# Three feed-forward tiles of the first 320 rows moved into the attention stage of a fused attention, Fourier-MLP and gated-MLP kernel

## The chip, the cores and the metric

The kernel runs on one core of one Trainium2 chip. The metric is the device time of one execution in microseconds (us); lower is better. Before the change the median of three runs is 816.88 us (815.56 to 817.01).

## What is computed

Three blocks follow each other, all in float32 on 4 sequences of 576 rows and 512 features.

```python
# 1. attention, 8 heads of 64, causal, window of 64 keys
scores = q @ k.T / 8, masked to 0 <= row - col < 64
x = softmax(scores) @ v                      # heads side by side: (4, 576, 512)
# 2. Fourier mixing and an MLP
u  = x + real(fft(fft(x, axis=1), axis=2))
un = (u - mean(u)) / sqrt(var(u) + 1e-6)
x  = u + maximum(un @ w_ch1, 0) @ w_ch2      # 512 -> 2048 -> 512
# 3. gated MLP with spatial mixing
h = gelu(x @ w_in); u, v = split(h)
v = w_sg @ layernorm(v) * g + b              # over the 576 rows of a sequence
out = x + (u * v) @ w_out
```

## The kernel before, in words

**Precision.** Wide products are made of three float32r matmuls: each operand is split into a high and a low part, and `mm3` (lines 113 to 120) issues high-high, high-low and low-high. Weights arrive from memory as 8-byte words and are turned into such pairs by `decode` (lines 142 to 161): a DMA into `dec_s`, then work on ScalarE (L154, L159), VectorE (L155 to L157) and GpSimd (L160). One tile `f` of the 16 feed-forward tiles is one `set`, decoded in four pieces. `set0` to `set2` are decoded beside the attention, the others later.

**Attention** (`attention`, lines 249 to 351) goes over 36 blocks of 64 queries, `n` = 9 per sequence. A block has scores (L260, into PSUM tile `sc`), a masked maximum on VectorE (L264), exponentials on ScalarE (L268), transposes (L275, into `pt`) and their copy (L277). Every two blocks there are the products with v (L288, into `pv`), the normalization on VectorE (L303 to L307), and a transpose back (L317, into `xt`) with a copy into `uT` (L319). The stages of several blocks overlap; `LAG` says by how many steps. PSUM has eight banks. In this stage two belong to tag `g` (Fourier transform and layernorm), two to `sc`, one to `pt`, one to `xt` and two to `pv`. The keys come in tiles of three blocks (`load_k`, three buffers), the values in tiles of two blocks (`load_v`, `VB` = 3 buffers). All these loads are issued by SyncE (SP), in one fixed order with the weight loads, so a load that waits for its buffer holds up the ones behind it.

**Beside the attention** run two lanes: the decoding of tiles 0 to 2, and per sequence `dft` (lines 380 to 461) and, for the row chunks 0 and 1, `ln` (lines 487 to 521). The 2304 rows are cut into eight chunks, `n` = 0 to 7, of 320 and 256 rows in turn. `ln` leaves a chunk's normalized rows transposed in `xh` and `xl` (L519, L520). Chunk 0 is the head of sequence 0, and is ready long before the attention ends; chunk 1 is the rest of sequence 0; chunk 2 needs the transform of sequence 1.

**The MLP** (`mlp`, lines 529 to 577) begins when the attention has released its memory. `PHASES` (lines 28 and 29) lists which feed-forward tiles are made for which chunks: for each pair, 12 matmuls make `h` from `xh`, `xl` and the first weight (L564), ScalarE and VectorE turn it into `rh`, `rl` (L568, L569), and 12 matmuls add into `acc` (L544). After the last tile of a phase VectorE adds `acc` to `uT` (L549, four instructions). Lane `rest` (lines 817 to 832) runs beside it: decoding of tile 3, layernorm of chunks 2 and 3, the transforms of sequences 2 and 3, layernorm of chunks 4 to 7. Then comes the gated MLP, which the change does not touch.

**What sets the order.** The Python generators are interleaved by `drive` (lines 728 to 743) by their estimated costs. The compiler layer then schedules all instructions per engine with its own model of their times, so the order on an engine differs from the order of the source. On the chip every engine executes its list strictly in that order.

## Time and profile before

| | us |
|---|---|
| median of three runs | 816.88 |
| the profiled execution: own time | 811.93 |
| the profiled execution: span, first to last instruction | 810.2 |
| attention, until the first matmul of the MLP | 147.9 |
| TensorE busy | 777.8 (96%) |
| VectorE busy | 478.2 (59%) |
| ScalarE busy | 290.9 (36%) |
| GpSimd busy | 163.5 (20%) |

The span is what the profile's views divide up; the profiled execution's own time is 1.7 us longer. PE is TensorE's matmul row, PEld its weight loads, which overlap the matmuls, DVE is VectorE, ACT ScalarE, POOL GpSimd, SP SyncE. A matmul's end is modelled in the profile, and matmuls overlap, so a PE that reads as busy all the time can still be less than full. An "idle before" in brackets is the time in which the engine waited just before an instruction, with the instruction that ended the wait.

### The profile page before, as it was taken

The page shows a single profiled execution, that of the slowest core. Times are in us where ns is not written, and L with a number is a line of the kernel's source. Part 1 is how long each engine was busy: PE and PEld are TensorE (multiplying, and loading weights), DVE is VectorE, ACT ScalarE, POOL GpSimd, SP SyncE. Part 2 cuts the span into 40 slices and gives each one's busy share as a digit, 9 for nine tenths or more (in the row PEclk, how much of TensorE's full clock was granted, in tenths as well). Part 3 has the DMA queues.
Part 4 walks back from the last instruction along what each step waited for, and adds up shares of the span by engine and source line. Part 5 has one row for each costly group of instructions (what it writes and reads, how often), then busy time and mean ns, then how long its engine had stood idle before and what let it go on. Part 6 is the DMA issues. An engine that isn't in the chain of part 4 may idle for free.

```text
span 810.2 us, 15611 instructions
## 1 busy us (share of the span) xinstructions
PE 777.8 (96%) x6084; PEld 748.4 (92%) x6084; DVE 478.2 (59%) x1390; ACT 290.9 (36%) x710; POOL 163.5 (20%) x202
## 2 busy tenths in 40 slices
PE   5979798899999999999999999999999999999998
PEld 5779597899998999999999999999999998989898
DVE  2688978996488557963226933643240258565653
ACT  3777776442233234431113411333242243131310
POOL 1143513442031013410002300232260021010100
PEclk8999999999999999999999999999999999999999
DMA  9997631121012003420002400132140020303032
GB/s 208 295 323 224 177 97 38 61 97 53 2 40 66 1 1 105 129 82 1 1 2 69 136 6 1 34 118 85 40 134 12 0 60 1 117 1 118 1 117 93
DMA packets 59321, 63.70 MB, mean 79 GB/s; under 512 B 22384, under 2 KB 42736, under 8 KB 59248
## 3 DMA queue, kind: packets, MB, share of 16 engines
q1 hardware_dynamic: 58672, 59.75, 24.9%
q0 software_dynamic: 576, 2.97, 1.2%
q8 instruction: 48, 0.79, 0.4%
q14 instruction: 25, 0.20, 0.1%
HBM read 53.25 MB, written 9.44 MB: 77 GB/s over the span
## 4 chain that ended last, share of the span: by engine, by line
PE 74%; DVE 14%; DMA 6%; ACT 2%; issue 2%; SPq 1%; POOL 1%; DVEq 0%; ACTq 0%
PE acc L118 7%; PE acc L119 7%; PE acc L120 7%; PE h L119 6%; PE h L120 6%; PE h L118 6%; PE c L119 6%; PE c L118 6%; PE c L120 6%; PE g L118 3%; PE g L119 3%; PE g L120 3%; DMA dec_s<-in_w 2%; PE sc L260 2%; DMA dec_s<-in_wo 2%
## 5 line engine op out<-in xcount | busy, mean ns | idle before, releaser
L118 PE MATMUL acc<-rh,set 128*128 128x256 f32 (+1 forms) x512 | 151.6, 296 | 2.2 <-DVE uT L549 2.1
L118 PE MATMUL h<-xh,set 128*128 128x256 f32 (+1 forms) x512 | 151.2, 296 | 0.8 <-DVE rl L569 0.8
L119 PE MATMUL acc<-rl,set 128*128 128x256 f32 (+1 forms) x512 | 151.3, 296 | 0.0
L120 PE MATMUL acc<-rh,set 128*128 128x256 f32 (+1 forms) x512 | 151.1, 295 | 0.0
L119 PE MATMUL h<-xl,set 128*128 128x256 f32 (+1 forms) x512 | 151.0, 295 | 0.0
L120 PE MATMUL h<-xh,set 128*128 128x256 f32 (+1 forms) x512 | 150.9, 295 | 0.0
L569 DVE SCALAR_TENSOR_TENSOR rl<-h,rh 128x320 fp32r<-128x320 f32 (+1 forms) x128 | 58.1, 454 | 118.1 <-ACT rh L568 117.6
L160 POOL TENSOR_TENSOR set<-dec_w,set 128x256 fp32r<-128x256 f32 x88 | 71.9, 823 | 253.7 <-ACT set L159 250.4
L568 ACT ACTIVATE rh<-h 128x320 fp32r<-128x320 f32 (+1 forms) x128 | 51.7, 404 | 161.2 <-PE h L120 121.3
L118 PEld LDWEIGHTS acc<-rh,set 128*128 128x128 f32 x512 | 96.4, 188 | 3.6 <-issue 1.3
L118 PEld LDWEIGHTS h<-xh,set 128*128 128x128 f32 x512 | 96.3, 188 | 1.7 <-DVE rl L569 1.3
L120 PEld LDWEIGHTS acc<-rh,set 128*128 128x128 f32 x512 | 96.5, 188 | 0.1
L119 PEld LDWEIGHTS h<-xl,set 128*128 128x128 f32 x512 | 96.4, 188 | 0.1
L120 PEld LDWEIGHTS h<-xh,set 128*128 128x128 f32 x512 | 96.4, 188 | 0.0
L119 PEld LDWEIGHTS acc<-rl,set 128*128 128x128 f32 x512 | 96.4, 188 | 0.0
L549 DVE TENSOR_TENSOR uT<-acc,uT 128x320 f32<-128x320 f32 (+1 forms) x160 | 62.0, 448 | 15.2 <-PE acc L120 15.2
L154 ACT ACTIVATE dec_g<-dec_s 128x256 f32<-128x256 f32 x88 | 38.4, 438 | 78.6 <-DVE dec_w L156 37.0
L268 ACT ACTIVATE s<-s,mx 128x128 f32<-128x128 f32 x144 | 46.9, 393 | 26.4 <-DVE mx L264 26.3
L482 POOL TENSOR_TENSOR rq<-rq,mhalf 128x1 f32<-128x1 f32 (+2 forms) x26 | 17.4, 669 | 189.9 <-DVE rq L481 186.8
L155 DVE TENSOR_SCALAR dec_w<-dec_s 128x256 int32<-128x256 int32 x88 | 34.8, 398 | 35.3 <-POOL set L160 23.1
L120 PE MATMUL c<-xh,set 128*128 128x256 f32 (+1 forms) x188 | 55.4, 294 | 0.0
L118 PE MATMUL c<-xh,set 128*128 128x256 f32 (+1 forms) x188 | 55.3, 294 | 0.0
(190 smaller groups left out, 1611.9 us busy)
## 6 DMA issues: line engine op xcount, KB each, us to landing
dec_s<-in_w SPq DMA_DIRECT2D x64, 256.0 KB, 2.8
v<-in_v SPq DMA_DIRECT2D x16, 520.0 KB, 6.0
k<-in_k SPq DMA_DIRECT2D x11, 512.0 KB, 6.5
dec_s<-in_wi SPq DMA_DIRECT2D x16, 256.0 KB, 2.8
q<-in_q SPq DMA_DIRECT2D x30, 128.0 KB, 5.4
x<-uT SPq DMA_DIRECT2D x4, 640.0 KB, 3.9
out<-uT SPq DMA_DIRECT2D x4, 640.0 KB, 3.9
dec_s<-in_wo SPq DMA_DIRECT2D x8, 256.0 KB, 2.5
```

The costliest lines, as they stand in the source:

```text
L118: mm(out, lhsT=lh, rhs=rh, start=first and i == 0, stop=False)
L119: mm(out, lhsT=lh, rhs=rl, start=False, stop=False)
L120: mm(out, lhsT=ll, rhs=rh, start=False, stop=last and i == n - 1)
L154: nc.scalar.activation(out=g, in_=s[:, :, 1].bitcast(F32), func=AF.Copy, scale=2.0 ** -112)
L155: nc.vector.tensor_scalar(out=w, in0=s[:, :, 0], scalar1=29, scalar2=None, op0=ALU.logical_shift_right)
L160: (eng or nc.gpsimd).tensor_tensor(out=lo[:, o:o + 256], in0=f, in1=hi[:, o:o + 256], op=ALU.subtract)
L260: nc.tensor.matmul(sc[:, hp], lhsT=q[:, hp].rearrange("p a b -> p (a b)"), rhs=k[:, hp, o:o + 128], start=True, stop=True)
L268: nc.scalar.activation(out=s[:, hp], in_=s[:, hp], func=AF.Exp, bias=mx[:, hp:hp + 1], scale=-1.0)
L482: self.nc.gpsimd.tensor_tensor(out=y, in0=v, in1=self.mhalf[:m, 0:n], op=ALU.pow)
L549: V.tensor_tensor(out=x, in0=acc[:, c, 0:size], in1=x, op=ALU.add)
L568: A.activation(out=rh, in_=o, func=AF.Relu)
L569: V.scalar_tensor_tensor(out=rl, in0=o, scalar=0.0, in1=rh, op0=ALU.max, op1=ALU.subtract)
```

## The change

Tiles 0 to 2 of chunk 0 leave the MLP. A new generator `early` makes them beside the attention once the layernorm of chunk 0 and the decoding of tiles 0 to 2 have been issued: for each tile 12 matmuls into a PSUM tile `e`, then the ScalarE and VectorE step into `erh`, `erl`; then for each of the four feature groups 9 matmuls into `e` and one VectorE addition to `uT`. `e` has one bank. That bank comes from the rings of the attention: `sc`, `pt` and `xt` now share one ring `ab` of three banks, where they had four. `erh` and `erl` take new memory (three buffers each), and the keys and values have two buffers each in place of three; `VL` = 3 issues a load of v one step later. In `PHASES`, chunks 1 to 3 now come first with tiles 0 to 3, then chunk 0 with tiles 3 to 5, then chunks 1 to 3 with tiles 4 and 5.

```diff
--- before.py
+++ after.py
@@ -25,17 +25,19 @@
 NCH = len(CHUNKS)
 P0 = 4
 HEAD, TAIL = range(NCH // 2), range(NCH // 2, NCH)
-PHASES = [(range(P0), HEAD), (range(P0, 6), HEAD), (range(P0), TAIL), (range(P0, 6), TAIL),
+E0 = range(3)
+PHASES = [(range(P0), HEAD[1:]), (range(3, 6), HEAD[:1]), (range(P0, 6), HEAD[1:]), (range(P0), TAIL), (range(P0, 6), TAIL),
           (range(6, 10), range(NCH)), (range(10, 13), range(NCH)), (range(13, 16), range(NCH))]
 URGENT = 5000
 SOON = 6000
 RATE = 1.0
 NV = 0
-VL = 2
-LAG, XPT = (1, 2, 3), 0
+VL = 3
+LAG = 1, 2, 3
 PACE = 1.0
+EC = 5
 FP = ()
-UB, SB, QB, VB = 3, 3, 3, 3
+UB, SB, QB, VB = 3, 3, 3, 2
 WARM, W0, W1 = 16, 9000, 2500
 TAB_AT = (2, 4, 7, 9)
 DSP, D45 = 2000, 3000
@@ -202,7 +204,7 @@
         self.kt, self.vt = {}, {}
 
     def load_k(self, b, g):
-        t = self.ap_.tile([128, 4, 256], F32, tag="k", bufs=3, name="k")
+        t = self.ap_.tile([128, 4, 256], F32, tag="k", bufs=2, name="k")
         o = 192 * g
         for c in (slice(0, 128), slice(128, 256)) if b == g == 0 else (slice(0, 256),):
             self.nc.sync.dma_start(t[:, :, c], self.aps["k"][b, :, :, o + c.start:o + c.stop])
@@ -254,7 +256,7 @@
         def scores(n):
             b, j = divmod(n, NB)
             q, k = self.qt.pop((b, j)), self.kt[b, j // 3]
-            sc = ps.tile([128, 4, 128], F32, tag="sc", bufs=2, name="sc")
+            sc = ps.tile([128, 4, 128], F32, tag="ab", bufs=3, name="sc")
             for hp in range(4):
                 o = 64 * (j % 3)
                 nc.tensor.matmul(sc[:, hp], lhsT=q[:, hp].rearrange("p a b -> p (a b)"), rhs=k[:, hp, o:o + 128], start=True, stop=True)
@@ -270,7 +272,7 @@
 
         def transposes(n):
             pr = st.pop(n)
-            pt = ps.tile([128, 4, 128], F32, tag="pt", bufs=1 + XPT, name="pt")
+            pt = ps.tile([128, 4, 128], F32, tag="ab", bufs=3, name="pt")
             for hp in range(4):
                 nc.tensor.transpose(pt[:, hp], pr[:, hp], self.ident)
             pts = p.tile([128, 4, 128], F32, tag="pts", bufs=3, name="pts")
@@ -312,7 +314,7 @@
             b, j = divmod(n, NB)
             m, x = 64 if j == NB - 1 else 128, st.pop(("x", n))
             i = j // 2
-            t = ps.tile([128, 4, 128], F32, tag="pt", bufs=2, name="xt") if XPT else ps.tile([128, 4, 128], F32, tag="xt", name="xt")
+            t = ps.tile([128, 4, 128], F32, tag="ab", bufs=3, name="xt")
             for c in range(4):
                 nc.tensor.transpose(t[:, c, 0:m], x[:m, 128 * c:128 * c + 128], self.ident[:m, :m])
             t0 = S * b + 128 * i
@@ -526,6 +528,30 @@
         self.bps, es = self.pool("mlp_ps", side="right", space=PSUM)
         self.mlp_es.enter_context(es)
 
+    def early(self, n, fs):
+
+        nc, p, ps = self.nc, self.ap_, self.aps_
+        start, size = CHUNKS[n]
+        xh, xl = self.xh[n], self.xl[n]
+        hid = {}
+        for f in fs:
+            t = self.sets[f % 8]
+            o = ps.tile([128, 512], F32, tag="e", name="e")[:, 0:size]
+            self.mm3(o, [(t[:, 0, 128 * k:128 * k + 128], t[:, 1, 128 * k:128 * k + 128], xh[:, k], xl[:, k]) for k in range(4)])
+            rh = p.tile([128, CA], F32R, tag="erh", bufs=len(fs), name="erh")[:, 0:size]
+            rl = p.tile([128, CA], F32R, tag="erl", bufs=len(fs), name="erl")[:, 0:size]
+            nc.scalar.activation(out=rh, in_=o, func=AF.Relu)
+            nc.vector.scalar_tensor_tensor(out=rl, in0=o, scalar=0.0, in1=rh, op0=ALU.max, op1=ALU.subtract)
+            hid[f] = rh, rl
+            yield EC * size
+        for c in range(4):
+            s = slice(128 * c, 128 * c + 128)
+            o = ps.tile([128, 512], F32, tag="e", name="e")[:, 0:size]
+            self.mm3(o, [(self.sets[f % 8][:, 2, s], self.sets[f % 8][:, 3, s], *hid[f]) for f in fs])
+            x = self.uT[:, c, start:start + size]
+            nc.vector.tensor_tensor(out=x, in0=o, in1=x, op=ALU.add)
+            yield EC * size
+
     def mlp(self, before):
         nc = self.nc
         V, A = nc.vector, nc.scalar
@@ -764,19 +790,26 @@
             for w in gen:
                 yield w * PACE
 
+        have = set()
+
         def work():
             for b in range(2):
                 yield from when(scaled(k.dft(b)), lambda: k.xdone >= b)
                 yield from scaled(k.ln(b))
+                have.add(b)
 
         def weights():
             yield W0
             for f in range(3):
                 yield from spaced(k.decode_f(f), W1)
+            have.add("w")
+
+        def early():
+            yield from when(k.early(0, E0), lambda: have >= {0, "w"})
 
         k.open_x(0, k.lp)
         k.open_x(1, k.lp)
-        fill = [[weights()], [work()]]
+        fill = [[weights()], [work()], [early()]]
         drive(k.attention(), *fill)
         for f in sum(fill, []):
             for _ in f:
@@ -854,14 +887,14 @@
                 next(rest_)
             if n == PHASES[g][1][0]:
                 drain(lanes[1])
-                if g == 3:
+                if g == 4:
                     lanes[1].append(decodes((8, 9), 2000))
-                elif g == 4:
+                elif g == 5:
                     drain(lanes[0])
                     lanes[1].append(decodes(range(10, 13), 7000))
-                elif g == 5:
+                elif g == 6:
                     lanes[1].append(decodes(range(13, 16), 5000))
-                elif g == 6:
+                elif g == 7:
                     lanes[1].append(w_in())
 
         drive(k.mlp(before), *lanes)
```

Three places show how the order moves. A line of the changed kernel has a number two higher than the same line before in these rows (its L120 is the L118 of before).

**TensorE in the attention stage, at the second transform.** `g` is the transform, `e` the early tiles, the rest attention. Before:

```order
L120 MATMUL g<-tab,ol 128x256
L260 MATMUL sc<-k,q_97 128x128 x4
L317 MATMUL xt<-ident,x 128x64 x2
L288 MATMUL pv<-v,pts 64x65
L317 MATMUL xt<-ident,x 128x64 x2
L275 MATMUL pt<-ident,s 128x128 x4
L288 MATMUL pv<-v,pts 64x65 x15
L118 MATMUL g<-tab,oh 33x256
```

After the change, where the scores of the same part of the stage are done:

```order
L277 MATMUL pt<-ident,s 128x128 x4
L290 MATMUL pv<-v,pts 64x65 x7
L120 MATMUL e<-erh,set_69 128x320
L121 MATMUL e<-erl,set_69 128x320
L122 MATMUL e<-erh,set_69 128x320
L120 MATMUL e<-erh,set_70 128x320
L121 MATMUL e<-erl,set_70 128x320
L122 MATMUL e<-erh,set_70 128x320
L120 MATMUL e<-erh,set_71 128x320
L121 MATMUL e<-erl,set_71 128x320
L122 MATMUL e<-erh,set_71 128x320
L290 MATMUL pv<-v,pts 64x65 x9
```

The nine matmuls of one `e` group stand in the middle of a `pv` run; nothing was there before.

**TensorE where chunk 2 begins.** `h` on `xh2` is the first product of chunk 2; `g` from `u` is the last transpose of its layernorm, `acc` the MLP's sum for chunk 1. Before, the transpose is followed by chunk 1:

```order
L119 MATMUL h_2701<-xl1_113,set3_2143 128x256
L120 MATMUL h_2701<-xh1_112,set3_2143 128x256
L517 MATMUL g_2514<-ident_58,u_2385 128x64 x4
L118 MATMUL h_2701<-xh1_112,set3_2143 128x256
L119 MATMUL h_2701<-xl1_113,set3_2143 128x256
L118 MATMUL g_2521<-tab_81,oh_2310 33x256
L119 MATMUL g_2521<-tab_81,oh_2310 33x256
```

After the change the same transpose is followed at once by chunk 2:

```order
L122 MATMUL g_2583<-tab_81,ol_2406 128x256
L120 MATMUL g_2583<-tab_81,oh_2405 128x256
L121 MATMUL g_2583<-tab_81,oh_2405 128x256
L122 MATMUL g_2583<-tab_81,ol_2406 128x256
L519 MATMUL g_2592<-ident_58,u_2480 128x64 x4
L120 MATMUL h_2619<-xh2_2234,set0_69 128x320
L120 MATMUL h_2698<-xh2_2234,set1_70 128x320
L120 MATMUL g_2599<-tab_81,oh_2405 33x256
```

Before, 37 other instructions stand between that transpose and the first product of chunk 2; now none do.

**SyncE's loads near the start.** Names are those of the tiles; `dec_s` is the first weight load. Before:

```order
L233 DMA v_141<-in_v 128x2x520
L208 DMA k_143<-in_k 128x4x256
L216 DMA q2_97<-in_q 64x8x64 x2
L233 DMA v_162<-in_v 128x2x520
L216 DMA q0_95<-in_q 64x8x64 x2
L208 DMA k_204<-in_k 128x4x256
L233 DMA v_206<-in_v 128x2x520
L216 DMA q1_96<-in_q 64x4x64 x2
L208 DMA k_311<-in_k 128x4x256
L151 DMA dec_s_313<-in_w1 128x512
```

After the change:

```order
L210 DMA k_141<-in_k 128x4x256
L235 DMA v_143<-in_v 128x2x520
L218 DMA q2_97<-in_q 64x8x64 x2
L235 DMA v_177<-in_v 128x2x520
L218 DMA q0_95<-in_q 64x8x64 x2
L210 DMA k_204<-in_k 128x4x256
L218 DMA q1_96<-in_q 64x4x64 x2
L153 DMA dec_s_313<-in_w1 128x512
L153 DMA dec_s_369<-in_w1 128x512
```

Between the load of `q0` and the first weight load, one load of v and one of k are gone from the queue; they come later.

## Rows read from the trace of the kernel before

**Rows 1.** Stretches: from:to, length, busy PE, PEld, DVE, ACT, POOL, clock, DMA share, GB/s:

```profile
25.00:104.00 79.00, 67.32 (x753) 58.90 (x753) 64.77 (x284) 57.91 (x164) 31.05 (x36) 1.00 0.83 243
104.00:148.00 44.00, 39.21 (x427) 34.30 (x425) 36.12 (x126) 26.95 (x70) 12.29 (x18) 1.00 0.24 71
148.00:180.00 32.00, 31.02 (x234) 29.74 (x233) 30.75 (x71) 16.36 (x44) 14.68 (x14) 1.00 0.25 80
180.00:300.00 120.00, 118.30 (x898) 115.45 (x897) 77.30 (x195) 36.94 (x85) 19.30 (x26) 1.00 0.10 28
300.00:780.00 480.00, 478.89 (x3455) 468.42 (x3454) 246.82 (x626) 138.31 (x313) 81.56 (x90) 1.00 0.18 56
```

**Rows 2.** The same view of two shorter stretches:

```profile
104.00:120.00 16.00, 16.00 (x182) 14.52 (x180) 11.15 (x52) 12.16 (x34) 1.91 (x4) 1.00 0.37 110
148.00:160.00 12.00, 11.55 (x86) 11.18 (x85) 12.00 (x28) 5.87 (x15) 5.06 (x4) 1.00 0.14 46
```

**Rows 3.** VectorE in order of time, layernorm's last step of chunks 1 and 2:

```profile
146.73 1.29 DVE L520 TENSOR_TENSOR xl<-g,xh 128x512 fp32r<-128x512 f32 x2 [0.57 <-ACT xh L519]
...
177.34 0.41 DVE L520 TENSOR_TENSOR xl<-g,xh 128x256 fp32r<-128x256 f32 x1
```

**Rows 4.** TensorE in order of time, first product of chunk 2:

```profile
179.92 0.31 PE L118 MATMUL h<-xh,set 128*128 128x320 f32 x1
```

**Rows 5.** TensorE in order of time, runs of 320 and of 256 columns, first and last:

```profile
148.11 0.31 PE L119 MATMUL h<-xl,set 128*128 128x320 f32 x1
...
149.57 0.31 PE L120 MATMUL h<-xh,set 128*128 128x320 f32 x1
...
177.00 0.28 PE L118 MATMUL acc<-rh,set 128*128 128x256 f32 x1
...
178.41 0.28 PE L118 MATMUL acc<-rh,set 128*128 128x256 f32 x1
```

**Rows 6.** Groups by line and shape, 0 to 260 us (xcount | busy, mean ns | idle before):

```profile
L568 ACT ACTIVATE rh<-h 128x320 fp32r<-128x320 f32 x13 | 5.6, 429 | 12.4 <-PE h L120 9.9 <-PE acc L120 2.5
L569 DVE SCALAR_TENSOR_TENSOR rl<-h,rh 128x320 fp32r<-128x320 f32 x13 | 6.3, 482 | 6.3 <-ACT rh L568 6.3
L549 DVE TENSOR_TENSOR uT<-acc,uT 128x320 f32<-128x320 f32 x16 | 6.7, 474 | 0.2 <-PE acc L120 0.2
```

**Rows 7.** Same view, the other VectorE steps whose count changes before chunk 2:

```profile
L569 DVE SCALAR_TENSOR_TENSOR rl<-h,rh 128x256 fp32r<-128x256 f32 x12 | 5.0, 419 | 2.2 <-ACT rh L568 2.2
L549 DVE TENSOR_TENSOR uT<-acc,uT 128x256 f32<-128x256 f32 x16 | 5.8, 412 | 1.1 <-PE acc L120 1.1
L155 DVE TENSOR_SCALAR dec_w<-dec_s 128x256 int32<-128x256 int32 x34 | 12.3, 369 | 4.4 <-DMA dec_s<-in_w 2.3 <-POOL set L160 2.1
L156 DVE SCALAR_TENSOR_TENSOR dec_w<-dec_g,dec_w 128x256 int32<-128x256 int32 x34 | 17.4, 515 | 1.6 <-ACT dec_g L154 1.3
L157 DVE SCALAR_TENSOR_TENSOR dec_w<-dec_s,dec_w 128x256 int32<-128x256 int32 x34 | 14.5, 431 | 0.2
```

**Rows 8.** VectorE in order of time, its two longest waits for a weight load:

```profile
30.54 0.29 DVE L155 TENSOR_SCALAR dec_w<-dec_s 128x256 int32<-128x256 int32 x1 [1.08 <-DMA dec_s<-in_w]
...
80.50 0.29 DVE L155 TENSOR_SCALAR dec_w<-dec_s 128x256 int32<-128x256 int32 x1 [1.20 <-DMA dec_s<-in_w]
```

**Rows 9.** TensorE in order of time, scores of blocks 1, 8, 27 and 29:

```profile
12.08 2.05 PE L260 MATMUL sc<-k,q 128*128 128x128 f32 x8 [5.41 <-DVE mx L264]
...
26.86 1.16 PE L260 MATMUL sc<-k,q 128*128 128x128 f32 x8
...
94.19 1.16 PE L260 MATMUL sc<-k,q 128*128 128x128 f32 x8 [1.65 <-DVE mx L264]
...
104.06 1.06 PE L260 MATMUL sc<-k,q 128*128 128x128 f32 x8
```

**Rows 10.** DMA issues: line, count, KB each, median us to landing:

```profile
v<-in_v SPq DMA_DIRECT2D x16, 520.0 KB, 6.0
k<-in_k SPq DMA_DIRECT2D x11, 512.0 KB, 6.5
```

## The prediction

> **What bounds the kernel now.** I read the busy times by stretch first. From 180 us to 780 us TensorE is busy for 118.3 of 120 and 478.9 of 480 us [rows 1]. It is the limit there, only 2.8 us are open, and the change leaves the work of that part as it is. So the end of the kernel moves by as much as the point near 180 us moves, and the question is what decides that point. The granted clock is 1.00 in every stretch from 25 us on, the 2.4 GHz level, so no term hangs on it.
>
> Before 180 us there are two kinds of stretch. In the attention neither engine is full: from 104 to 148 us TensorE is busy for 39.2 of 44 us, VectorE for 36.1, and TensorE's weight loads for 34.3 [rows 1]. Short steps hand work from engine to engine there. From 148 to 180 us, the start of the MLP, VectorE is busy for 30.75 of 32 us and TensorE for 31.0, so both are full at once. In its first part, 148 to 160 us, VectorE is busy for all 12.00 us, and in the fullest part of the attention, 104 to 120 us, TensorE reads as busy for 16.00 of 16 us while its weight loads take 14.52 [rows 2].
>
> The point that matters is where chunk 2 enters the MLP. VectorE finishes chunk 1 at 146.73 + 1.29 = 148.0 us and the last piece of chunk 2 at 177.34 + 0.41 = 177.75 us [rows 3]. The first product of chunk 2 starts at 179.9 us [rows 4], 2.2 us after it could. That slack is small.
>
> **The change, part by part.** *What moves.* 3 x 12 matmuls for h and 4 x 9 for the sums, 72 of 320 columns. One takes 0.146 us: ten steps from 148.11 to 149.57 us [rows 5]. That is 10.5 us of TensorE, out of the MLP and into the attention. With them go 3 relus on ScalarE (3 x 0.429 = 1.3 us), and on VectorE 3 low parts and 4 additions, 3 x 0.482 + 4 x 0.474 = 3.3 us [rows 6]. Nothing is computed twice, and the number of additions to uT over the whole kernel stays the same.
>
> *What the attention pays.* The early tiles need the layernorm of chunk 0, so they fall into the stretch from 104 us on. I measure it by the weight loads, the lower of TensorE's two readings: 34.3 + 10.5 = 44.8 us. Filled as densely as the long MLP stretch (468.4 of 480, 97.6%), that takes 45.9 us, and the attention ends 1.9 us later. As sparse as it is now (34.3 of 44, 78%), it takes 57.4, and it ends 13.4 us later. I take the density of its own fullest part, 14.52 of 16 = 91%: 49.2 us, 5.2 later. The early work is independent of the attention's chains and fills their gaps, but it stands in a strict list between them.
>
> *The single bank.* A group in `e` cannot begin before the one ahead of it has been read. Six boundaries cost at most 3 x (0.429 + 0.482) + 3 x 0.474 = 4.1 us [rows 6], if nothing stands between, and nothing if VectorE is prompt. In the new order other matmuls stand between all of them, but VectorE has a queue of its own. I take a third, 1.4 us. The attention then ends 5.2 + 1.4 = 6.6 us later, against 10.5 us saved: TensorE alone would win 3.9 us.
>
> *What takes it back.* With chunk 0 gone from the first phase, chunk 2 comes sooner after the start of the MLP, and its layernorm does not. It depends on VectorE's list between chunk 1 and chunk 2, which took 177.75 - 148.0 = 29.7 us almost without a gap. In the new order this list is shorter by 1.5 us of low parts (4 x 0.482 + 3 x 0.419 become 4 x 0.419), 0.25 us of additions (4 x 0.474 become 4 x 0.412) and 2.2 us of decoding (2 x 0.369 + 2 x 0.515 + 0.431), 4.0 us in all [rows 7]. So chunk 2 is ready 25.7 us after chunk 1, and TensorE arrives there well ahead: it has only 96 products of 256 columns for chunk 1, at 1.41 / 12 = 0.1175 us [rows 5] 11.3 us, and 53 others of the transform and layernorm. In the new order the first product of chunk 2 follows the last transpose of its layernorm with nothing between. It starts at 148.0 + 6.6 + 25.7 = 180.3 us, where it was 179.9.
>
> Is as much work done at that point? Before, 24 sums of chunk 1 were still to do (2.8 us); now they are done, but 24 matmuls of chunk 0's tile 3 are to do (24 x 0.146 = 3.5 us). That adds 0.7 us. The sum: 180.3 + 0.7 - 179.9 = **1.1 us later**. As a rule of thumb the end moves by X - 5.5 us, where X is how much later the attention ends.
>
> *The start.* With fewer buffers, one load of v and one of k, 1.0 MB, no longer stand ahead of the first weight load. VectorE waited 1.08 and 1.20 us for such loads [rows 8], so at most 2.3 us are to be won. On the other side stand the shared ring and the later loads, the second and fourth rivals below. I take nothing for the start and keep both ends. SyncE executes its list in order, so a k that waits for its buffer holds the q, v and weight loads behind it, and VectorE's list stops at the decoding.
>
> The profiled execution took 811.93 us, 4.95 us below the median of 816.88; I add the difference to the median: **818.0 us**. About 0.2% (1.6 us) is what a measurement of this kernel can tell from no change, so this is within it, on the slow side.
>
> **The rivals.** *First: the attention packs well, faster.* The weight loads leave 9.7 of the 44 us open, enough for nearly all 10.5. At 97.6% X is 1.9 and the end moves by -3.6: 813.3 us; with the 2.3 us of the start 811.0. For it: VectorE is idle for 8 us in the same stretch, so both engines have room. Against it: the room was there before too and stayed at 78%, and chunk 2 still waits for VectorE. By TensorE's busy row (39.2) only 4.8 us would be open, X could not be under 5.7, and this rival would be out. The Trainium skill, page "Perfetto Trace Analysis", section "Identifying the Most-Contended Engine", says that matmul busy time is a poor measure of headroom and weight-load time a good one. The trace agrees in the 16 us where the one is at 100% and the other at 91%, and by that rule this rival stays in.
>
> *Second: the score bank, slower.* In the order of the source, five tiles per two blocks (two scores, two transposes, one xt) go round three banks, so the scores of every second block can start only when VectorE has read those of the block before; with two banks of their own they wait for the block before that one. Even so TensorE met such a wait, 1.65 us at 94.19 [rows 9]. While it lasts VectorE works, but after it VectorE has nothing to reduce until the eight score matmuls are through, 1.06 us at 104.06 [rows 9]. For 18 such blocks that is at most 19 us. VectorE has other work in most of them; if a quarter is bare, it costs 4.8 us: 822.8. It makes the change slower from 0.5 us bare on.
>
> *Third: the single bank is not covered.* Then all 4.1 us count, X is 9.3 and the time is 820.7. For it: VectorE is busy for 82% of the stretch, so a read seldom starts at once. The Trainium skill, same page, section "Optimizing Tensor Performance", says that independent matmul groups should rotate through different PSUM banks so that one group's evacuation overlaps the next group's matmuls; this change does the opposite with `e`. Rows here show the price of one evacuation, not how much is bare.
>
> *Fourth: k and v come late.* A load of v takes 6.0 us and one of k 6.5 [rows 10]. From block 8 (26.86) to block 29 (104.06) a block takes 3.7 us [rows 9], so the two blocks of the other v buffer last 7.4 us and cover it. From block 1 (12.08) to block 8 a block takes 2.1 us, two last 4.2: each of four tiles can be 1.8 us late, 7.2 in all. With a third of that on the path, 2.4 us: 820.4.
>
> That the change doesn't do what it says is no case: the new order shows the early matmuls in the attention.
>
> **How the numbers follow.** The forecast (X from 4.2, at the 93% of 148 to 160 us with a prompt bank, to 8.0 with two thirds of the bank's price; 815.6 to 819.4) gets 0.39; the first rival 0.29; the second 0.15; the third 0.11; the fourth 0.06. Faster by over 0.2%: 0.28 of the first rival and 0.01 of the forecast's own edge, 0.29. Within 0.2%: 0.25 of the forecast, 0.01 of the first and 0.02 of the fourth, 0.28. Slower: 0.13 of the forecast, 0.15, 0.11 and 0.04 of the fourth, 0.43. The range goes from 811.5, almost the best of the first rival, to 823.0, just over the second.
>
> **What would show it.** Right: the last low part of chunk 1 ends 5 to 8 us later than 148.0; the first product of chunk 2 starts within 2 us of 179.9 and waits for VectorE's or ScalarE's part of its layernorm; VectorE is busy for over 90% between the two; the weight loads are at about 91% from 104 us on; from there to the end TensorE has no new gaps. Wrong: the first product of chunk 2 starts at 178 us or before (first rival), or the block scores show many waits of 1 us or more for VectorE's reads or for k and v (second and fourth), or the first matmuls of `e` groups do (third). If chunk 2 starts on time and the end still moves, the forecast's first step, that nothing changes behind 180 us, is wrong.

## The result and the profile after

The changed kernel takes 824.17 us (820.34 to 825.51, 7 runs), the kernel before beside it 815.56 (814.12 to 817.01, 7 runs): ratio 1.0104 with a 95% interval of 1.0086 to 1.0122. It is slower by about 1%, and above the range that was forecast. That is 8.6 us between the medians. The profiled execution has a span of 822.4 us, 12.2 more than before: it is the median one, while that of the kernel before is a fast one (811.93 us, 3.6 below the median beside it). Two executions lie far off, one of the kernel before with 858.27 us and one of e10_kv_list with 1937.84 us, and the ratios, though not the medians, leave them out.

The stretches of [rows 1] in the changed kernel (from:to, length, busy PE, PEld, DVE, ACT, POOL, clock, DMA share, GB/s):

```profile
25.00:104.00 79.00, 64.56 (x649) 56.88 (x649) 62.72 (x256) 53.09 (x144) 27.57 (x34) 0.91 0.78 216
104.00:148.00 44.00, 43.65 (x417) 39.64 (x418) 29.74 (x111) 24.03 (x65) 10.63 (x13) 1.00 0.39 103
148.00:180.00 32.00, 28.58 (x272) 25.49 (x270) 27.40 (x81) 18.01 (x45) 10.58 (x12) 1.00 0.13 42
180.00:300.00 120.00, 114.14 (x849) 110.78 (x848) 85.20 (x210) 41.39 (x100) 26.27 (x33) 0.97 0.14 45
300.00:780.00 480.00, 479.48 (x3459) 469.32 (x3458) 246.14 (x627) 140.70 (x318) 81.78 (x90) 1.00 0.17 53
```

From 104 to 148 us TensorE is nearly full and its weight loads stand at 39.64 of 44, which is 90%; the forecast took 91%. New is the first row: less is done on every engine before 104 us, and the granted clock, 1.00 before, is 0.91. VectorE's rows that answer to [rows 3], chunks 0, 1 and 2:

```profile
110.14 0.69 DVE L522 TENSOR_TENSOR xl<-g,xh 128x512 fp32r<-128x512 f32 x1
...
163.70 1.29 DVE L522 TENSOR_TENSOR xl<-g,xh 128x512 fp32r<-128x512 f32 x2 [0.25 <-ACT xh L521]
...
190.55 0.42 DVE L522 TENSOR_TENSOR xl<-g,xh 128x256 fp32r<-128x256 f32 x1
```

TensorE in order of time: the longest wait of the start, and the rows that answer to [rows 4]:

```profile
54.46 0.58 PE L425 MATMUL g<-tab,grow 128*128 128x258 f32 x1 [4.10 <-DVE grow L406]
...
186.79 0.63 PE L519 MATMUL g<-ident,u 128*128 128x128 f32 x4 [1.71 <-DVE xl L522]
189.06 0.69 PE L519 MATMUL g<-ident,u 64*128 64x64 f32 x4
190.22 0.90 PE L120 MATMUL h<-xh,set 128*128 128x320 f32 x2 [0.47 <-ACT xh L521]
```

The first low part of chunk 0 (the layernorm's last step, `xl`) starts at 110.14 us; in the kernel before it starts at 104.05. Chunk 1 is complete at 164.99, where it was 148.02: X, in the words of the forecast, is 17.0 us, not 6.6. Of it 6.1 us arise ahead of chunk 0, in the start, and 10.9 between chunk 0 and chunk 1 (54.85 us, before 43.97). Behind chunk 1 things go as forecast: the first product of chunk 2 follows 25.2 us later. The four pieces sum up: 6.1 + 10.9 - 6.7 (25.2 for 31.9 us) + 1.9 (632.2 for 630.3 us from there to the end) = 12.2 us. The 6.1 us are the least certain: e17_k2_list below has the lists of before and its time, and in its profiled execution, 0.1 us from its median, chunk 0 starts at 106.63 us. Against that the start of the change loses 3.5 us.

### The profile page after: what moved, and what is told of

Its sections match the earlier page's. It is cut to its first block, busy times and chain, and to the rows that moved or that the text cites. A ratio compares the mean times of both kernels' runs of the same rounds, so it can differ in the third digit from the quotient of the medians.

```text
span 822.4 us, 15628 instructions
## 1 busy us (share of the span) xinstructions
PE 788.3 (96%) x6084; PEld 757.5 (92%) x6084; DVE 480.5 (58%) x1390; ACT 293.5 (36%) x710; POOL 162.0 (20%) x202
## 4 chain that ended last, share of the span: by engine, by line
PE 84%; DVE 9%; DMA 3%; ACT 2%; issue 1%; SPq 0%; POOL 0%; ACTq 0%; DVEq 0%
PE acc L120 7%; PE h L120 7%; PE acc L121 7%; PE acc L122 7%; PE h L122 7%; PE h L121 7%; PE c L121 6%; PE c L120 6%; PE c L122 6%; PE g L120 3%; PE g L121 3%; PE g L122 3%; PE sc L262 3%; PE pv L290 2%; DVE E L392 2%
## 5 line engine op out<-in xcount | busy, mean ns | idle before, releaser
L120 PE MATMUL h<-xh,set 128*128 128x256 f32 (+1 forms) x500 | 147.9, 298 | 2.7 <-DVE rl L595 2.2
L121 PE MATMUL acc<-rl,set 128*128 128x256 f32 (+1 forms) x500 | 147.5, 295 | 1.3 <-DVE rl L595 1.3
L120 PE MATMUL acc<-rh,set 128*128 128x256 f32 (+1 forms) x500 | 147.9, 296 | 0.5 <-DVE uT L575 0.4
L121 PE MATMUL h<-xl,set 128*128 128x256 f32 (+1 forms) x500 | 147.8, 296 | 0.0
L122 PE MATMUL h<-xh,set 128*128 128x256 f32 (+1 forms) x500 | 147.5, 295 | 0.0
L122 PE MATMUL acc<-rh,set 128*128 128x256 f32 (+1 forms) x500 | 147.4, 295 | 0.0
L595 DVE SCALAR_TENSOR_TENSOR rl<-h,rh 128x256 fp32r<-128x256 f32 (+1 forms) x125 | 56.6, 453 | 121.2 <-ACT rh L594 121.0
L594 ACT ACTIVATE rh<-h 128x256 fp32r<-128x256 f32 (+1 forms) x125 | 50.5, 404 | 168.5 <-PE h L122 119.9
L120 PEld LDWEIGHTS h<-xh,set 128*128 128x128 f32 x500 | 94.5, 190 | 3.3 <-DVE rl L595 2.6
L120 PEld LDWEIGHTS acc<-rh,set 128*128 128x128 f32 x500 | 94.2, 188 | 1.1 <-issue 1.0
L122 PEld LDWEIGHTS h<-xh,set 128*128 128x128 f32 x500 | 94.7, 189 | 0.0
L122 PEld LDWEIGHTS acc<-rh,set 128*128 128x128 f32 x500 | 94.2, 188 | 0.1
L575 DVE TENSOR_TENSOR uT<-acc,uT 128x256 f32<-128x256 f32 (+1 forms) x156 | 60.4, 448 | 15.1 <-PE acc L122 15.1
L120 PE MATMUL c<-xh,set 128*128 128x256 f32 (+1 forms) x188 | 55.3, 294 | 0.0
L121 PE MATMUL c<-xl,set 128*128 128x256 f32 (+1 forms) x188 | 55.3, 294 | 0.0
```

Of the source, the lines that this page charges most:

```text
L120: mm(out, lhsT=lh, rhs=rh, start=first and i == 0, stop=False)
L121: mm(out, lhsT=lh, rhs=rl, start=False, stop=False)
L122: mm(out, lhsT=ll, rhs=rh, start=False, stop=last and i == n - 1)
L575: V.tensor_tensor(out=x, in0=acc[:, c, 0:size], in1=x, op=ALU.add)
L594: A.activation(out=rh, in_=o, func=AF.Relu)
L595: V.scalar_tensor_tensor(out=rl, in0=o, scalar=0.0, in1=rh, op0=ALU.max, op1=ALU.subtract)
```

## The experiments

Each further kernel was timed in five rounds beside the kernel before, whose median was 814.7 to 815.8 us in the five batches. The table gives the ratio and, from the profiled execution, when the first low part of chunk 0 starts and when chunk 1 is complete. "Lead" is counted in TensorE's list: how many blocks the scores are ahead of the transposes, on average over the points where a PV (the products with v) or an xt begins, as long as scores are left to do.

| kernel | time, us | ratio (95%) | chunk 0 | chunk 1 | lead |
|---|---|---|---|---|---|
| before | 815 | 1 | 104.05 | 148.02 | 3.28 |
| the change | 824.17 | 1.0104 (1.0086-1.0122) | 110.14 | 164.99 | 1.07 |
| e1_ring | 828.35 | 1.0172 (1.0146-1.0198) | 114.36 | 163.38 | 1.13 |
| e2_kv | 820.01 | 1.0062 (1.0041-1.0083) | 115.89 | 157.79 | 3.40 |
| e3_ring_kv | 826.98 | 1.0134 (1.0094-1.0174) | 112.65 | 160.91 | 1.10 |
| e6_late2 | 825.7 | 1.0132 (1.0100-1.0165) | 105.00 | 159.90 | 1.07 |
| e7_fill | 825.4 | 1.0127 (1.0104-1.0150) | 110.73 | 165.57 | 1.07 |
| e4_gbank | 837.73 | 1.0280 (1.0249-1.0311) | 118.47 | 184.16 | 3.20 |
| e9_ptxt | 831.35 | 1.0190 (1.0161-1.0220) | 113.67 | 171.93 | 3.65 |
| e8_v2 | 825.07 | 1.0121 (1.0096-1.0145) | 109.73 | 153.50 | 3.32 |
| e10_kv_list | 822.36 | 1.0079 (1.0047-1.0110) | 114.02 | 158.00 | 3.28 |
| e11_before_e3list | 824.58 | 1.0117 (1.0088-1.0146) | 107.35 | 157.03 | 1.10 |
| e12_g_list | 831.6 | 1.0191 (1.0168-1.0214) | 110.50 | 169.53 | 3.28 |
| e13_draw | 813.99 | 0.9978 (0.9961-0.9996) | 105.78 | 152.05 | 3.21 |
| e14_after_draw | 829.13 | 1.0163 (1.0138-1.0189) | 107.32 | 175.08 | 1.12 |
| e15_after_draw2 | 821.84 | 1.0076 (1.0056-1.0097) | 103.98 | 161.42 | 1.07 |
| e16_v2_list | 822.64 | 1.0083 (1.0052-1.0114) | 114.55 | 158.52 | 3.28 |
| e17_k2_list | 814.67 | 0.9994 (0.9978-1.0010) | 106.63 | 150.61 | 3.28 |
| e18_v3 | 827.18 | 1.0141 (1.0117-1.0166) | 114.84 | 168.31 | 1.13 |
| e19_v3_draw2 | 831.01 | 1.0188 (1.0166-1.0210) | 107.72 | 166.14 | 1.13 |

The columns of chunk 0 and chunk 1 are of one execution each. The start varies: the change and e6_late2 have the same lists up to chunk 1, and chunk 0 comes 5.1 us apart. TensorE waits 3.9 us for v in the one (2.09 us at 30.61 and 1.79 at 41.57) and not at all in the other. Under the same lists the stretch from chunk 0 to chunk 1 is steady: 43.97 to 43.98 us in before, e10_kv_list and e17_k2_list, 54.84 to 54.90 in the change, e7_fill and e6_late2. Steps of the start are read from the ratios.

### One part of the change at a time

**e1_ring**: the shared ring alone, on the kernel before.

```diff
-            sc = ps.tile([128, 4, 128], F32, tag="sc", bufs=2, name="sc")
+            sc = ps.tile([128, 4, 128], F32, tag="ab", bufs=3, name="sc")
```

(The same edit for pt and xt is left out here.)

> The kernel before with one edit: sc, pt and xt share one ring of three banks; k and v keep three buffers, no early tiles, one bank stays unused. The layernorm of chunk 0 ended about 7 us later in the changed kernel (first xl at 111.2 us against 104.05). Theory A (the shared ring makes the attention slower): this run is 4 to 8 us slower than before, with the first xl of chunk 0 at 108 us or later. Theory B (the loads in two buffers do it): within 1.5 us of before, first xl of chunk 0 at 103 to 106 us. Theory C (neither alone, only together): also within 1.5 us, and e3 tells it from B.

(The 111.2 us here and in e7_fill is the second low part of chunk 0; the first starts at 110.14.)

**e2_kv**: k and v in two buffers alone, with the v loads three blocks behind.

```diff
-VL = 2
+VL = 3
-UB, SB, QB, VB = 3, 3, 3, 3
+UB, SB, QB, VB = 3, 3, 3, 2
-        t = self.ap_.tile([128, 4, 256], F32, tag="k", bufs=3, name="k")
+        t = self.ap_.tile([128, 4, 256], F32, tag="k", bufs=2, name="k")
```

> The kernel before with one edit: k and v in two buffers and VL = 3; the rings as before, no early tiles. Theory A (the shared ring): within 1.5 us of before. Theory B (the loads): 4 to 8 us slower than before, with waits of TensorE for v or k of 1 us or more near the start and the first xl of chunk 0 at 108 us or later. Theory C (only together): within 1.5 us.

**e3_ring_kv**: both edits, no early tiles.

> Both edits of e1 and e2, no early tiles: the changed kernel's attention without what it makes room for. Its order on VectorE is that of the changed kernel up to the layernorm of chunk 0. All theories put the first xl of chunk 0 near 111 us. If the price of the room is all of the loss at the start, the run is about 7 us slower than before (A and B: the sum of e1 and e2; C: much more than the sum). If the 7 us come from the half clock that follows TensorE's gaps, the granted clock is under 0.95 between 25 and 104 us here as well.

**e6_late2**: the change, with tiles 3 to 5 of chunk 0 between chunk 1 and chunk 2, to give VectorE's list time.

```diff
-PHASES = [(range(P0), HEAD[1:]), (range(3, 6), HEAD[:1]), (range(P0, 6), HEAD[1:]), (range(P0), TAIL), (range(P0, 6), TAIL),
+PHASES = [(range(P0), HEAD[1:2]), (range(3, 6), HEAD[:1]), (range(P0), HEAD[2:]), (range(P0, 6), HEAD[1:]), (range(P0), TAIL), (range(P0, 6), TAIL),
```

(Left out: four places further down count the phases, and count one more.)

> The changed kernel with one edit: the phase of chunk 0 with tiles 3 to 5 stands between chunk 1 and chunk 2, so chunk 2 comes 72 matmuls later in TensorE's list; attention as in the changed kernel. In the changed kernel TensorE waits 6.3 us in five waits between 170 and 191 us, mostly for chunk 2's layernorm, and its clock is halved at 190 to 195 us. Theory D (VectorE's list up to chunk 2 takes the early work back): the waits go, and the run is 4 to 8 us faster than the changed kernel, 816 to 820 us. Theory E (only the length of the attention counts, what is lost at chunk 2 would be lost elsewhere, since VectorE has the same work to do before the second half): within 1.5 us of the changed kernel, 822.5 to 825.5 us.

The ring alone loses 13.5 us, the two buffers 5.2, both 12.1: in these runs they do not add. Each has lists of its own, though. The scheduler draws up other lists at the least edit, and three such draws of the change lie 7 us apart (e14_after_draw and e15_after_draw2 below), so the missing 6.6 us prove little. The early tiles are not the loss: with them the ratio is 1.0104, without them 1.0134, and the intervals overlap. Work between chunk 1 and chunk 2 gains nothing (e6_late2), which fits the forecast's rule that the end moves with chunk 1. The stretch from chunk 0 to chunk 1 before:

```profile
104.05:148.02 43.97, 39.18 (x426) 34.27 (x425) 36.14 (x126) 26.90 (x69) 12.31 (x18) 1.00 0.24 71
```

The stretches from 25 us to chunk 0 and from there to chunk 1 of e3_ring_kv, then of the change; up to the first early tile the two have the same lists on all four engines:

```profile
25.00:112.65 87.65, 72.65 (x727) 63.28 (x728) 66.98 (x281) 57.33 (x157) 29.95 (x37) 0.92 0.78 206
112.65:160.91 48.26, 42.95 (x452) 38.03 (x451) 35.36 (x132) 29.85 (x79) 13.39 (x17) 1.00 0.36 97
```

```profile
25.00:110.14 85.14, 70.70 (x716) 62.17 (x716) 67.11 (x282) 56.98 (x155) 29.61 (x37) 0.92 0.75 208
110.14:165.00 54.86, 53.30 (x514) 47.30 (x513) 38.16 (x140) 30.32 (x79) 11.82 (x17) 1.00 0.32 86
```

Ring and buffers lengthen the second stretch from 43.97 to 48.26 us; it holds 452 matmuls for 426, so a part of this is work that came late out of the start. The early tiles add 54.86 - 48.26 = 6.6 us. TensorE is then busy for 53.30 of the 54.86 us, its weight loads for 47.30, which is 86%.

### Is it the clock?

In the start of the change TensorE's clock is down to the 1.2 GHz level behind three of its waits; in the profiled execution of the kernel before it never is from 25 us on. **e7_fill** keeps every list and puts transposes of the identity into the waits, to the unused bank `e`:

```diff
+FILL = {("g", 1): 26, ("pv", 2): 13, ("xt", 10): 13}
+    insert(nc)
```

(`insert`, left out here, puts so many transposes ahead of the first matmul of that tile.)

> The changed kernel with every instruction of every engine in the same order, and 52 transposes of the constant identity more on TensorE, written to the bank `e` before anything uses it and read by nobody: 13 ahead of the PV that waits 2.09 us for v at 30.6 us, 26 ahead of the product that waits 4.10 us for `grow` at 54.5 us, 13 ahead of the transposes that wait 2.16 us for `x` at 95.5 us. Each wait is as long as its filling (about 0.15 us a transpose), so the filling itself should cost nothing. Theory C (much of the late start is the 1.2 GHz level that follows these three waits): granted clock 1.00 at 30 to 36, 51 to 60 and 96 to 102 us, the first low part of chunk 0 at 105 to 108 us instead of 111.2, and 818 to 821 us in all. Theory L (the waits themselves and the lists' order cost, the clock falls beside them and costs nothing): low part at 111 to 112 us, 824 to 825 us.

The change and e7_fill (same columns as the stretches above):

```profile
30.00:36.00 6.00, 5.39 (x55) 5.09 (x56) 2.00 (x11) 2.62 (x8) 1.70 (x4) 0.72 1.09 299
51.00:60.00 9.00, 5.54 (x30) 5.38 (x32) 6.82 (x19) 4.52 (x14) 3.57 (x4) 0.62 0.55 167
96.00:102.00 6.00, 6.00 (x55) 5.04 (x54) 5.42 (x27) 3.73 (x10) 1.54 (x2) 0.72 0.38 78
```

```profile
30.00:36.00 6.00, 5.42 (x68) 4.67 (x66) 3.18 (x20) 4.38 (x15) 2.24 (x4) 1.00 1.13 269
51.00:60.00 9.00, 7.87 (x88) 7.15 (x84) 8.62 (x30) 6.00 (x16) 3.60 (x5) 1.00 0.73 232
96.00:102.00 6.00, 4.87 (x53) 3.49 (x51) 5.94 (x31) 5.53 (x15) 2.24 (x2) 1.00 0.30 71
102.00:108.00 6.00, 4.79 (x38) 3.88 (x40) 3.75 (x16) 2.50 (x9) 1.55 (x3) 0.72 0.52 179
```

The clock stays up in all three places and falls once, later, at 102 to 108 us. Neither chunk 0 (110.73 us) nor the time (825.4 us) comes sooner, so Theory C of this run, which expected 818 to 821 us, is out. That the low clock is free does not follow. Three rows of VectorE, in the change and then in e7_fill:

```profile
52.85 0.76 DVE L407 TENSOR_TENSOR O<-O 128x576 f32<-128x576 f32 x1
...
63.47 0.29 DVE L266 CUSTOM_DVE_ANT_0 s<-sc,mask 128x128 f32<-128x128 f32 x1
...
103.07 0.69 DVE L309 TENSOR_TENSOR x<-pv,rd 128x512 f32<-128x512 f32 x1
```

```profile
54.09 0.76 DVE L407 TENSOR_TENSOR O<-O 128x576 f32<-128x576 f32 x1
...
62.67 0.29 DVE L266 CUSTOM_DVE_ANT_0 s<-sc,mask 128x128 f32<-128x128 f32 x1
...
102.39 0.68 DVE L309 TENSOR_TENSOR x<-pv,rd 128x512 f32<-128x512 f32 x1
```

This execution of e7_fill is 1.2 us late at the first row and 0.8 us early at the second: where the clock stayed up it gained 2.0 us. At the third, an `x` for which TensorE waits 2.3 us, it is 0.7 us early, and at the first low part of chunk 0 it is 0.6 us late again, with TensorE's clock down in between. So e7_fill gained 2.0 us where it kept the clock up and lost 1.3 where the clock fell next. What the low clock costs in all stays open. It is not the loss of the change, for the five executions of e7_fill have a mean granted clock of 0.985 to 0.992, the kernel before beside them 0.987 to 0.993, and still the medians are 825.4 and 814.87 us.

### Which sharing, and other places for the early tiles

**e4_gbank**: the change with the rings of before, early tiles in the ring `g`.

```diff
-            o = ps.tile([128, 512], F32, tag="e", name="e")[:, 0:size]
+            o = self.gtile()[:, 0:size]
```

(Left out: the same edit at the second such line, and the tags of sc, pt and xt as before.)

> The changed kernel with the rings of before (two banks for scores, one for pt, one for xt) and the early tiles through the two banks of the ring `g` instead of a bank of their own; k and v stay in two buffers. Theory A (sharing three banks among scores, probabilities and x is what costs, 13.5 us alone): 815 to 818 us, that is the 820.0 of the two buffers alone less the 3 us that the early tiles gained against ring and buffers without them. Theory B (two buffers for k and v and the moved work cost, the ring only shifts lists): 821 to 825 us. A third outcome, that early tiles in `g` hold up the DFT and the layer norms: above 825 us.

**e9_ptxt**: the change with two banks for scores and one for pt and xt together.

```diff
-            sc = ps.tile([128, 4, 128], F32, tag="ab", bufs=3, name="sc")
+            sc = ps.tile([128, 4, 128], F32, tag="sc", bufs=2, name="sc")
-            pt = ps.tile([128, 4, 128], F32, tag="ab", bufs=3, name="pt")
+            pt = ps.tile([128, 4, 128], F32, tag="ab", bufs=1, name="pt")
```

(Left out: xt like pt.)

> The changed kernel with two banks for scores as before, and one bank shared by pt and xt (before: one each); the bank `e`, two buffers and the early tiles as in the change. Theory A1 (what costs in the shared ring is that scores take banks and run ahead, so that TensorE stands before `grow` and `x`): 817 to 821 us. Theory A2 (one bank for pt and xt is what costs, since a block's transposes then wait for the copy of the other): 825 to 830 us.

**e8_v2**: before with v alone in two buffers.

```diff
-VL = 2
+VL = 3
-UB, SB, QB, VB = 3, 3, 3, 3
+UB, SB, QB, VB = 3, 3, 3, 2
```

> Before with v in two buffers and loaded three blocks behind q and k, and k in three as before. If v is what costs in the pair of two buffers (820.0 us, 5.2 over before): 819 to 821 us. If k is: 814 to 816 us. If the order that each edit gives the lists decides and not the buffers: anything, with TensorE waits of 2 to 4 us and half clock behind them where it is slower.

All three came out at or beyond the worst that was expected, and e8_v2, with more room than e2_kv, is slower than it (1.0121 for 1.0062). In e4_gbank TensorE stands for 13.4 us at transposes of the layernorm in `g` that wait for VectorE's `u`, 12.2 of them in one wait; in e9_ptxt it waits 8.5 us where pt stands behind ScalarE's copy of xt, or xt behind that of pt. Since each edit also makes the scheduler draw other lists, such pairs do not tell room from order. The next four do.

### Room or lists

Here TensorE's, VectorE's, ScalarE's and GpSimd's lists up to the end of the attention are forced to be those of another kernel, by dependences that order without a wait:

```diff
+        pin(tc)
```

(`pin`, left out here, ties on each of the four engines every instruction to the one ahead of it in the recorded list.)

**e10_kv_list**: e2_kv with the lists of before.

> Before with k and v in two buffers (the edit that took 820.0 us against 814.85), but with the lists of TensorE, VectorE, ScalarE and GpSimd up to the end of the attention forced to be those of before, instruction for instruction; only SyncE's list is the scheduler's. Theory O (the edits cost because they make the scheduler draw up other lists; the room itself is hardly needed): 813 to 817 us, first low part of chunk 0 at 103 to 106 us, TensorE's waits for v and k under 1 us in all. Theory R (the room is needed, the engines wait for loads that come later): 818 to 823 us, with waits for v, k or dec_s of 2 us and more.

**e11_before_e3list**: before, all its room, with the lists of e3_ring_kv.

> The reverse: before with all its room (two banks for scores, one for pt, one for xt; three buffers for k and v), but with the lists of TensorE, VectorE, ScalarE and GpSimd up to the end of the attention that the scheduler drew up for the shared ring with two buffers and no early tiles (826.98 us). Theory O (lists): 824 to 829 us, first low part of chunk 0 at 110 us or later, in spite of the room. Theory R (room): 813 to 818 us. Between the two: both count, in the proportion that the time shows.

**e12_g_list**: e4_gbank with the lists of before, only the early tiles inserted.

> The changed kernel with the rings of before, the early tiles through the ring `g`, k and v in two buffers, and the lists of before forced up to the end of the attention, so that only the early tiles are inserted (36 products right behind the layer norm of chunk 0, the other 36 in four pieces). Without forced lists it took 837.7 us. Theory O: the start is that of before (low part of chunk 0 at 103 to 106 us), the 10.5 us of products lengthen the attention by 6 to 9 us, and chunk 2 follows 25 us behind chunk 1: 814 to 819 us, so between 1 us faster and 4 us slower than before. Theory R (two buffers and the missing bank cost by themselves): 821 us or more.

**e13_draw**: before, other lists in the same room.

```diff
-PACE = 1.0
+PACE = 1.1
```

> Before with one number changed that takes no room: the transform and layer norms of the first two sequences are handed to the scheduler a tenth later in the program (PACE 1.1 for 1.0). About a hundred rows of VectorE's list change places, no bank, buffer or instruction does. Theory O: another draw of the lists, and so some other time; 817 to 825 us if the list of before is a lucky or well tuned one. Theory R: 813 to 817 us, as nothing is taken away.

Both count. The lists drawn for three banks and two buffers lose 9.4 us even where all room is there (e11_before_e3list), against 12.1 with the room gone. The two intervals overlap, so what the room itself adds under these lists is not shown, nor how the 9.4 us divide between ring and buffers. It is not that any new list is worse: e13_draw is no slower than before. And e10_kv_list shows room: its stretch from chunk 0 to chunk 1 is that of before to 0.01 us, but chunk 0 comes 10 us later, and its ratio is 1.0079. Its two stretches, and TensorE's waits for v:

```profile
25.00:114.02 89.02, 73.87 (x765) 65.41 (x764) 66.81 (x286) 58.85 (x164) 29.57 (x36) 0.92 0.79 214
114.02:158.00 43.98, 39.19 (x426) 34.24 (x425) 36.15 (x126) 26.91 (x69) 12.32 (x18) 1.00 0.32 89
```

```profile
31.47 0.30 PE L288 MATMUL pv<-v,pts 128*64 128x65 f32 x2 [1.46 <-DMA v<-in_v]
...
38.49 0.30 PE L288 MATMUL pv<-v,pts 128*64 128x65 f32 x2 [3.10 <-DMA v<-in_v]
```

How the ring's lists differ can be read in them. TensorE's list near block 11, before and then the change, without the PV (sc_610 are the scores of one block, s_616 the same block's probabilities, pt_690 their transposes):

```
L260 MATMUL sc_610<-k_311,q0_95 128x128 x4
L275 MATMUL pt_581<-ident_58,s_502 128x128 x3
L260 MATMUL sc_675<-k_470,q0_95 128x128 x4
L317 MATMUL xt_604<-ident_58,x_553 128x128 x4
L260 MATMUL sc_731<-k_470,q1_96 128x128 x4
L275 MATMUL pt_641<-ident_58,s_562 128x128 x4
L260 MATMUL sc_787<-k_470,q1_96 128x128 x4
L317 MATMUL xt_648<-ident_58,x_601 128x64 x4
L275 MATMUL pt_690<-ident_58,s_616 128x128 x4
```

```
L262 MATMUL sc_610<-k_309,q0_95 128x128 x4
L277 MATMUL pt_639<-ident_58,s_560 128x128 x4
L319 MATMUL xt_646<-ident_58,x_601 128x64 x4
L262 MATMUL sc_673<-k_468,q0_95 128x128 x4
L277 MATMUL pt_690<-ident_58,s_616 128x128 x4
```

Before, three further blocks' scores stand between a block's scores and its transposes; in the change it is one. Every kernel with the ring or with its lists has a lead of 1.07 to 1.13, every other 3.2 to 3.65. Why the scheduler does so is argued: five tiles per two blocks go round three banks in the order of the source, which leaves no bank for scores far ahead. Three banks under the lists of before were not tried. The expectations for e9_ptxt and e14_after_draw had it the wrong way round ("scores run ahead"). With a short lead VectorE would have no reductions in hand when it needs a PV. Its waits from 9 to 150 us, before (first two) and e11_before_e3list, with the same banks (engine, waiting, for whom: us in total, times, longest):

```profile
DVE s L264 <- PE sc L260: 8.5, 4, 3.5
...
DVE rc L303 <- PE pv L288: 2.8, 3, 1.2
```

```profile
DVE rc L303 <- PE pv L288: 8.8, 9, 1.9
DVE s L264 <- PE sc L260: 8.7, 9, 1.9
```

In the change it is 7.5 us in 8 waits for PV, in e1_ring 14.4 in 10. But e2_kv, with a lead of 3.40, has 9.0 us in 7 of them, and e9_ptxt, with 3.65, has 8.7 in 5. So e11_before_e3list shows that these lists lose time, and that they lose it by the short lead is argued, not shown. In e12_g_list the lead is that of before, but the 36 products of `h` stand in one piece behind the layernorm, VectorE waits 6.5 us for relus, and the stretch grows to 59.0 us.

### The ring or this draw, v or k, and the sum

**e14_after_draw** and **e15_after_draw2**: the change with `PACE` 1.1 and 0.9.

> The changed kernel with the transform and layer norms of the first two sequences handed to the scheduler a tenth later (PACE 1.1), the edit that cost before nothing (814.0 us). If the late chunk 1 is the accident of one draw of the lists: 814 to 820 us, the last low part of chunk 1 by 158 us. If every list for three shared banks is of the kind (scores run ahead, products and x behind, VectorE waits 7 to 9 us in all for products of PV): 822 to 828 us, last low part of chunk 1 at 162 us or later.

> The same with the transform a tenth sooner (PACE 0.9), a third draw of the changed kernel's lists. Accident of one draw: at least one of the two draws is under 820 us. The ring: both are 822 to 828 us.

**e16_v2_list**: e8_v2 with the lists of before. **e17_k2_list**: k alone in two buffers, with the lists of before.

```diff
-        t = self.ap_.tile([128, 4, 256], F32, tag="k", bufs=3, name="k")
+        t = self.ap_.tile([128, 4, 256], F32, tag="k", bufs=2, name="k")
```

> Before with v in two buffers, loaded three blocks behind q and k, and all lists but SyncE's forced to be those of before. With both k and v in two buffers this took 822.4 us, with TensorE waiting 4.6 us for v. If v is the buffer that is missed: 820 to 823 us, with those waits. If k is: 814 to 817 us.

> Before with k alone in two buffers (v in three, loaded two blocks behind as before) and all lists but SyncE's forced to be those of before. If k is the buffer that is missed: 819 to 823 us, with scores that wait 2 us and more. If v is: 814 to 817 us.

**e18_v3**: the change with v in three buffers again and, for the room, two early tiles; tile 2 goes back behind the attention (its line in `PHASES` is left out here). **e19_v3_draw2**: the same with `PACE` 0.9.

```diff
-E0 = range(3)
+E0 = range(2)
-VL = 3
+VL = 2
-UB, SB, QB, VB = 3, 3, 3, 2
+UB, SB, QB, VB = 3, 3, 3, 3
```

> The changed kernel with v in three buffers and loaded two blocks behind, as before; k stays in two; to make room two early tiles instead of three (tile 2 goes back behind the attention). If the two causes add: the third v buffer takes 5 to 8 us off, 816 to 820 us, a third of the early tiles' gain lost within it. If they do not add (the start is set by whichever of late loads and late products is worse, and with the ring the products are): 823 to 829 us, near the 828.35 of the ring alone less 2 us for the early tiles.

> The same in the draw that was the better one for the changed kernel (PACE 0.9, 821.84 with v in two buffers and three early tiles). If the causes add: 814 to 818 us, and this would be the version to set against before (814.65). If they do not: 820 to 825 us.

The draw of the change's lists is worth 7 us (821.84 to 829.13), but no draw has a median under 821 us. Of the two buffers, v is the one that the lists of before need: 822.64 without it, 814.67 without the third k, a difference of 8.0 us. That edit takes a buffer and also issues the load a step later (`VL` = 3); the two were not tried apart. Under the ring's lists the third v buffer brings nothing back in the two draws that were tried (827.18 and 831.01), with one early tile fewer. That a start made late by the short lead hides the late v would fit, and is argued, not shown: TensorE did wait 3.9 us for v in one execution of the change's lists and not in another, 5.1 us sooner at chunk 0. Why e18_v3 and e19_v3_draw2 are slower than the change stays open. No version here beats the kernel before by more than the 0.2% of e13_draw, which is that kernel in another draw.

## Why the prediction was wrong

**The step that failed: "I take nothing for the start and keep both ends".** It set the shared ring and the later loads at nothing, and they are the loss. Without the early tiles they take 12.1 us by the medians of e3_ring_kv. In the profiled executions the start lost 6.1 us (3.5 against e17_k2_list), and ring and buffers 4.3 us more between chunk 0 and chunk 1 (e3_ring_kv, 48.26 for 43.97), where the forecast had no term for them either. X was 17.0 us for the 6.6 forecast. The 2.3 us to be won by fewer loads ahead of the weights were not won: VectorE still waits 1.7 us for a weight load, for the 1.08 and 1.20 of [rows 8].

**The second rival named the cause, the ring, and not how it costs.** It had a chance of 0.15 and a price of 4.8 us. Measured: 13.5 us for the ring alone, in one draw. It priced scores that wait for a bank while the engines run, and looked at TensorE's wait at 94.19 [rows 9]; no such wait is left. The lists drawn for the three banks give up the lead instead. That the price stands in the lists is shown by e11_before_e3list alone, where it stays when the banks come back; that it is the lead in them is argued. The new order was there to be read ahead of the run; the prediction read in it where the early products stand and not how far the scores lead.

**The fourth rival**, k and v late, is real and was under-priced: 2.4 us of 7.2. It is v, buffer and later issue together, and it is 8.0 us under the lists of before. What it takes in the change is not shown: the kernel with ring and two buffers is no slower than that with the ring alone (826.98 for 828.35), yet TensorE waits 3.9 us for v in the profiled execution of the change.

**The attention's own price came out, in part by luck.** It was 6.6 us for the 72 products and the single bank; between e3_ring_kv and the change it is 6.6 us too. But that is one draw: in the other two draws of the change the stretch from chunk 0 to chunk 1 is 57.43 and 67.76 us (e15_after_draw2, e14_after_draw), for 54.86. The weight-load density of 91% was 90% from 104 to 148 us and 86% over the stretch itself. The reading by TensorE's busy time (X not under 5.7) would have done as well. The third rival is out: no first matmul of an `e` group waits for an evacuation. The Trainium skill advises to rotate groups through banks (page "Perfetto Trace Analysis", section "Optimizing Tensor Performance"). Here `e` does not rotate, 24 and more other matmuls stand between its groups, and it shows no loss; the 13.5 us of e1_ring are no test of the advice, since that ring does rotate.

**What takes it back held too.** Chunk 2 follows chunk 1 by 25.2 us for 25.7 forecast, VectorE busy for 24.69 of them, and with X = 17.0 the rule X - 5.5 gives 11.5 for 12.2 measured. "Nothing changes behind 180 us" is right but for 1.2 us over the 0.7 forecast: TensorE, busy for 1.61 us between 186 and 189, goes on at a granted clock of 0.50 from 189 to 195 us, which may be where they come from.

**"No term hangs on the clock"** was read from an execution that never left the upper level from 25 us on. In e17_k2_list, with the same lists, the granted clock is 0.53 from 53 to 60 us, and VectorE, 1.41 us ahead of that execution at the decoding row at 58.21 us (56.80 there), is 0.05 us behind it at 62.22 (62.27). So the clock has a price here, also with the lists of before. That it is not the loss of the change, e7_fill shows by its mean clock.

## What to carry to other kernels

Where a scheduler draws up the lists, a bank or buffer that is taken away can cost by waits (v here, under unchanged lists) or by the lists that are drawn without it (the ring here); compare in the new order how far producers lead consumers, above all on the engine that feeds the others, and take a difference there for a lead to follow and not for proof. Forcing one kernel's lists on another kernel's room tells the two apart in two runs, and a redraw in unchanged room gives the noise of drawing: 0.2% for the kernel before, 7 us for the change. Price work that moves into a stretch and the room that it needs there as separate terms: here the first came out within the spread of the draws, and the second was the result. And see whether the one profiled execution is a typical one before a small term is read from it.

## What the runs showed that was not expected

In the change three waits of TensorE, of 2.09, 4.10 and 2.16 us, stand beside a clock at the lower level. Filling them with idle transposes kept the clock at 1.00 (51 to 60 us: 0.62 against 1.00) and gained 2.0 us there. The kernel was not faster for it: the clock fell at a later wait, and 1.3 us were lost there (e7_fill). Two executions with the same lists reached chunk 0 5.1 us apart (110.14 and 105.00), 4.7 of it by the first fold `E` at 45.94 and 41.25 us.
